# Another written-out order for a one-core attention and expert kernel

## The chip, the cores and the metric

The kernel runs on one core of a Trainium2 chip. A core has a matrix engine (TensorE, PE in the profile; its weight loads are PEld), VectorE (DVE), ScalarE (ACT), GpSimd (POOL) and SyncE (SP). Each works through its own instructions in order; between engines, instructions wait for semaphores. Transfers between the off-chip memory and the on-chip memory (SBUF) are started by instructions on SP, on POOL or on ScalarE, and run by themselves. TensorE writes its results to PSUM, which has eight banks here called P0 to P7. The metric is the device time of one execution in microseconds; lower is better.

## The reference

With 8 batches, 12 heads, 448 rows and a head width of 64:

```
scores = (q @ k^T) / sqrt(64)
attn   = max(scores, 0)**2 / 448
x      = (attn @ v), heads side by side        # 3584 x 768
h      = x @ w_in                              # 3584 x 2048
g      = h / (1 + exp(-1.702 h))
out    = g @ w_out                             # 3584 x 768, float32
```

All inputs are float32; the kernel computes its products in float16 with float32 sums.

## The kernel before, in words

The attention is cut into 24 units (a batch and four heads), numbered 0 to 23. The rest is cut into eight groups of tokens, g = 0 to 7, of 384 and 512 tokens in turn. A group can start when the units of its tokens are done. Most of the work of groups 1 to 7 uses a scheme with seven products in place of eight (Strassen's), which needs sums and differences of blocks: of w_in (`winS`), of w_out (`wT`), of x (`T`) and of g (`asum`).

The order of everything is written out by hand, as a list of 1950 words. The kernel reads the list from front to back and issues each word's instructions; each engine then runs its own in that order. A word has a name, numbers, after `:` the engine that does it (a ScalarE, d VectorE, p POOL), and after `@` the PSUM banks that it takes. Without a suffix `K`, `r`, `t` and `h` are on ScalarE, `Q` and `v` on POOL, and the others on VectorE (`home`). The words that matter here, with the lines of the code that they run:

- `Lk8`, `Lq8`: load k or q of unit 8 in float32 into `kst` / `qst` (one buffer each), on SP's queue (L99). `K8`, `Q8`: the cast to float16. `Rk8`, `Rq8`: a transposition by DMA on SP's queue into `kT` / `qT` (three tiles each, L119). `jk`, `jq`, `V`: a load that casts on the way, on POOL's queue (L104). In units 0 to 5, `tk`, `tq` transpose on TensorE instead (L131) and `ek`, `eq` copy the result.
- `s8.3`: the scores of block 3 of unit 8, four matmuls into two banks (L150). `r8.3.0`, `r8.3.1`: relu of the two banks into a float16 tile `at` (L161 on VectorE, L163 on ScalarE). `x8.3`: the square of that tile in place, 128 x 896 (L169 on ScalarE, L88 on VectorE or POOL). `a8`: attention times v for the whole unit, 28 matmuls, four for each of the seven blocks in order (L181). `e`: copies of its result into x.
- `jwa`, `jwb`, `jo`: loads of w_in and w_out, on POOL's queue. `S`, `W`, `T`, `A`: the sums of w_in, w_out, x and g, on VectorE (L88). All four read two tiles in SBUF.
- `f`: the plain first product of group 0 and part of group 1 (L228). `u`: one of the seven products for a block of w_in and a group, six matmuls into the banks `hx` (L203). `t`: a copy of such a bank into a float32 tile `gf` (five buffers, L79 or L83). `b`: bank plus `gf`. `g`: the activation into `gf` (ScalarE, L214). `v`: the step that scales `gf` and writes it as float16 into `ge` or `go` ("widen", L217).
- `p`: one of the seven products with w_out, eight matmuls into the banks `ox` (L203); `i`: a single of 16 matmuls for the odd tile of a group. `h`, `l`, `n`: copies and sums of their results into `osb`; `l` with last number 5 is a plain copy. `o`, `q`: stores.

A word that waits for its data holds up every later word on its engine, and on that engine alone. On POOL stand only words that read SBUF, and transfers.

## Time and profile before

| | |
|---|---|
| time, median of 3 runs | 368.98 us (368.62 to 369.25) |
| the profiled execution | span 372.2 us; the profile gives no other time for it |
| mean granted TensorE clock in it | 0.987 |
| busy time PE / DVE / ACT / POOL | 358.6 / 302.9 / 281.3 / 137.6 us |
| HBM read / written | 45.61 / 11.01 MB |
| last block of w_out landed | 66.2 us after the start |

The profile is one execution with every instruction's start and end on each engine. Besides a page with totals it answers questions: groups of instructions by line, engine and shapes (count, busy time, mean duration in ns, idle time before them and what ended it), who waited for whom, the chain of work that ended last, instructions in order of time, and the busy time of each engine in given stretches, followed there by the granted clock, the DMA share and GB/s. In the page's picture of 40 equal slices (9.3 us each) a digit is the busy share in tenths.

### The profile page before, as it was taken

To read this page: it belongs to the slowest core of one execution; us is meant where nothing else is said; L and a number is where in the kernel's file an instruction comes from. 1 tells how busy PE (TensorE), PEld (TensorE's weight loads), DVE (VectorE), ACT (ScalarE), POOL (GpSimd) and SP (SyncE) were. 2 spreads that over 40 slices of the span, in tenths; PEclk is the share of its full clock that TensorE was granted. 3 is DMA by queue.
4 is the path that set the end of the run, shared out by engine and by line. 5 is a ranking of instruction groups with operands and counts; after the bars stand their busy time and mean duration, and the time that the engine had idled before them with its cause. 6 is when DMAs were issued, how large, how long until landed. Compare 5 with 4: busy or idle time off the path is not lost.

```text
span 372.2 us, 9025 instructions
## 1 busy us (share of the span) xinstructions
PE 358.6 (96%) x3562; PEld 233.2 (63%) x3562; DVE 302.9 (81%) x556; ACT 281.3 (76%) x540; POOL 137.6 (37%) x202
## 2 busy tenths in 40 slices
PE   7699999799999999999999999999999999999994
PEld 4345554465559755786558755686559755688562
DVE  3988995899988989877998889898897899856552
ACT  3979985579989998798897898868887889346210
POOL 5859264714412732054411613344602421034300
PEclk9989999899999999999999999999999999999998
DMA  9999999918997791849965695784583242300334
GB/s 192 183 204 163 213 209 226 218 18 173 200 225 165 151 221 25 167 105 174 179 170 98 146 184 172 188 171 119 82 205 23 41 97 26 85 2 2 85 97 117
DMA packets 65226, 51.38 MB, mean 138 GB/s; under 512 B 35744, under 2 KB 61856, under 8 KB 65184
## 3 DMA queue, kind: packets, MB, share of 16 engines
q1 hardware_dynamic: 48176, 36.22, 43.2%
q0 software_dynamic: 16608, 14.09, 26.4%
q8 instruction: 28, 0.46, 0.5%
q10 hardware_dynamic: 400, 0.49, 0.4%
q14 instruction: 14, 0.11, 0.1%
HBM read 45.61 MB, written 11.01 MB: 152 GB/s over the span
## 4 chain that ended last, share of the span: by engine, by line
PE 84%; DMA 7%; DVE 3%; POOL 2%; ACT 1%; issue 1%; SPq 0%; DVEq 0%; ACTq 0%
PE ox L203 30%; PE hx L203 27%; PE sc L150 9%; PE av L181 8%; PE os L203 6%; DMA wout<-in_moe_w_out_dram 4%; PE ht L228 3%; DMA v<-in_v_dram 2%; DMA qst<-in_q_dram 1%; DVE wT L88 1%; PE tr L131 1%; POOL ge L217 1%; DVE at L88 1%; ACT gf L214 1%; POOL go L217 0%
## 5 line engine op out<-in xcount | busy, mean ns | idle before, releaser
L163 ACT ACTIVATE at<-sc 128x448 f16<-128x448 f32 x201 | 99.6, 559 | 13.0 <-PE sc L150 12.7
L161 DVE TENSOR_SCALAR at<-sc 128x448 f16<-128x448 f32 x135 | 79.8, 618 | 10.9 <-PE sc L150 10.6
L217 POOL TENSOR_SCALAR go<-gf 128x512 f16<-128x512 f32 x64 | 42.6, 665 | 79.1 <-ACT gf L214 75.7
L169 ACT ACTIVATE at<-at 128x896 f16<-128x896 f16 x72 | 68.2, 962 | 1.7 <-DVE at L161 1.2
L217 POOL TENSOR_SCALAR ge<-gf 128x384 f16<-128x384 f32 x64 | 35.4, 554 | 74.0 <-ACT gf L214 70.8
L203 PEld LDWEIGHTS <-win 128*128 128x128 f16 x624 | 56.7, 98 | 8.5 <-issue 2.4
L88 DVE TENSOR_TENSOR at<-at 128x896 f16<-128x896 f16 x92 | 55.9, 631 | 1.7 <-ACT at L163 0.6
L88 DVE TENSOR_TENSOR gf<-hx,gf 128x512 f32<-128x512 f32 (+1 forms) x78 | 47.7, 625 | 11.5 <-ACT gf L79 5.4
L150 PE MATMUL sc<-qT,kT 64*64 64x448 f16 x672 | 52.6, 363 | 1.3 <-DVE qT L83 0.6
L214 ACT ACTIVATE gf<-gf 128x512 f32<-128x512 f32 (+1 forms) x78 | 43.8, 585 | 11.7 <-DVE gf L88 11.6
L203 PEld LDWEIGHTS <-winS 128*128 128x128 f16 x468 | 43.4, 99 | 8.2 <-issue 3.9
L203 PE MATMUL ox<-wout,go 128*128 128x384 f16 x256 | 46.4, 326 | 0.0
L203 PEld LDWEIGHTS <-go 128*128 128x128 f16 x320 | 29.9, 98 | 23.2 <-issue 5.8
L203 PE MATMUL hx<-T,winS 128*128 128x256 f16 (+1 forms) x312 | 38.2, 268 | 2.7 <-DVE gf L83 2.7
L181 PE MATMUL av<-at,v 64*64 64x448 f16 x672 | 37.5, 357 | 1.0 <-DMA v<-in_v_dram 1.0
L203 PEld LDWEIGHTS <-ge 128*128 128x128 f16 x256 | 24.0, 98 | 18.4 <-issue 4.1
L150 PEld LDWEIGHTS <-kT 64*64 64x64 f16 x672 | 18.7, 106 | 26.3 <-issue 22.1
L79 ACT ACTIVATE gf<-hx 128x384 f32<-128x384 f32 (+1 forms) x44 | 23.3, 537 | 15.4 <-PE hx L203 12.0
L203 PE MATMUL ox<-wT,asum 128*128 128x384 f16 x192 | 34.9, 327 | 0.0
L203 PE MATMUL hx<-xo,win 128*128 128x256 f16 x252 | 31.4, 273 | 0.4 <-ACT gf L79 0.4
L203 PEld LDWEIGHTS <-asum 128*128 128x128 f16 x224 | 21.1, 98 | 16.3 <-issue 3.3
L81 ACT ACTIVATE osb<-ox 128x384 f32<-128x384 f32 x32 | 15.4, 496 | 19.2 <-PE ox L203 19.1
(75 smaller groups left out, 475.9 us busy)
## 6 DMA issues: line engine op xcount, KB each, us to landing
out_dram<-osb SPq DMA_DIRECT2D x52, 192.0 KB, 3.2
kst<-in_k_dram SPq DMA_DIRECT2D x19, 448.0 KB, 4.7
qst<-in_q_dram SPq DMA_DIRECT2D x19, 448.0 KB, 4.9
v<-in_v_dram POOLq DMA_DIRECT2D x24, 224.0 KB, 5.6
win<-in_moe_w_in_dram POOLq DMA_DIRECT2D x8, 384.0 KB, 9.7
wout<-in_moe_w_out_dram POOLq DMA_DIRECT2D x4, 768.0 KB, 11.5
...
```

Source lines behind the costliest of these rows:

```text
L79: nc.scalar.activation(out=o, in_=i, func=AF.Copy)
L81: nc.scalar.activation(out=o, in_=i, func=AF.Copy, scale=scale)
L88: eng[e].tensor_tensor(out=o, in0=x, in1=y, op=op)
L150: nc.tensor.matmul(out=sc[a][c, 0:S], lhsT=st["kT"][r, j, c], rhs=st["qT"][r, :, c], start=True, stop=True)
L161: nc.vector.tensor_scalar(out=o, in0=i, scalar1=0.0, scalar2=None, op0=ALU.max)
L163: nc.scalar.activation(out=o, in_=i, func=AF.Relu)
L169: nc.scalar.activation(out=at, in_=at, func=AF.Square)
L181: nc.tensor.matmul(out=av[s][64 * a:64 * a + 64, 0:S], lhsT=v16[r, a, 64 * j:64 * j + 64], rhs=at[r, a, :], start=(j == 0), stop=(j == J - 1))
L203: nc.tensor.matmul(out=o, lhsT=lhs(i), rhs=rhs(i), start=start and i == 0, stop=i == n - 1, skip_group_check=True)
L214: nc.scalar.activation(out=o, in_=i, func=AF.Gelu_apprx_sigmoid, scale=1.0 / SC)
L217: eng[e].tensor_scalar(out=o, in0=i, scalar1=SC, scalar2=1.0, op0=ALU.mult, op1=ALU.mult)
L228: nc.tensor.matmul(out=hp[g, f][:, 0:n], lhsT=w[:, i, fo:fo + 128], rhs=xts[g][:, i, 0:n], start=i == 0, stop=i == NK - 1)
```

## The change

The list of words is replaced by another list of the same 1950 words. Each name with its numbers is there exactly once in both. What differs is the order, the engine suffixes and the bank numbers. No operation is added or taken out, and no tile changes its size or its number of buffers.

By engine suffix, the words that change most are these:

| word | before | after |
|---|---|---|
| `x` square (168) | 92 VectorE, 72 ScalarE, 4 POOL | 58 VectorE, 42 ScalarE, 68 POOL |
| `r` relu (336) | 201 ScalarE, 135 VectorE | 212 ScalarE, 124 VectorE |
| `v` widen (128) | 128 POOL | 92 POOL, 36 VectorE (19 of 384 columns, 17 of 512) |
| `K` cast (19) | 7 ScalarE, 3 VectorE, 9 POOL | 4 ScalarE, 3 VectorE, 12 POOL |
| `Q` cast (19) | 9 POOL, 9 ScalarE, 1 VectorE | 4 POOL, 9 ScalarE, 6 VectorE |
| `l` 5 copy (12) | 8 ScalarE, 4 VectorE | 1 ScalarE, 11 VectorE |
| `e` copy of attention (72) | 40 ScalarE, 32 VectorE | 38 ScalarE, 34 VectorE |

Of the four loads of w_out, `jo0.0`, `jo0.1`, `jo1.1`, `jo1.0` is the order before; after, it is `jo1.0`, `jo0.0`, `jo1.1`, `jo0.1`, and the last two stand later in the list. Of the first loads, `V0` and `V1` stand ahead of `jwb2`.

The diff, cut to the stretches that are spoken of (lines of the list between them left out):

```diff
@@ -465,182 +465,180 @@
         two["z"] = zeros
         words = (
-            "jq1 z13@0 Lk0 I K0:d tk0@1 ek0 z1 Lq0 Q0:a tq0@2 tq1@3 jk1 eq0 s0.1@4.5 jwb2 jk2 "
-            "s0.6@6.7 s0.4@0.1 r0.4.0:d r0.6.0 tk1@2 ek1 jq2 jq3 eq1 s0.3@6.0 r0.1.1 r0.4.1 "
-            "r0.1.0 x0.1 s0.0@5.2 r0.0.0 s0.2@1.4 r0.2.0:d r0.3.1:d r0.3.0 s0.5@3.5 r0.6.1 "
-            "s1.1@6.1 r0.2.1 r0.0.1:d s1.2@7.0 s1.5@4.2 x0.0 r0.5.0 r1.1.1 r1.2.1 jk3 x0.4 "
-            "r0.5.1:d tq2@3 r1.2.0 x0.2 x0.6:a x0.5 x0.3 V0 r1.5.1 s1.0@1.0 x1.2 tk2@7 r1.5.0:d "
-            "r1.0.0 ek2 tk3@5 r1.0.1 jwa0 s1.3@2.1 eq2 r1.1.0 x1.1:a V2 a0@0.6 V1 x1.5:a r1.3.1 "
-            "s1.4@4.7 ek3 r1.3.0 jq4 jwb0 s2.1@3.5 r1.4.1 e0.0.1 s2.2@1.2 r1.4.0:d jk4 e0.0.0 "
...
-            "r3.3.0 r3.2.0 f0.3.1 V3 ek4 f0.2.1 f0.0.0@6 s3.0@5.3 a2@2.7 e2.0.0 r3.0.0 S2.1 "
-            "r3.0.1 x3.0:a e2.0.1:a s3.1@4.5 r3.1.0 f0.1.0@3 f0.0.1 f0.1.1 f0.1.2 e2.1.0:a g0.1 "
...
-            "s4.6@4.6 s4.4@7.5 jo0.0 eq5 f0.10.0@0 r4.4.0:d f0.10.1 f0.10.2 x4.0 v0.8 e3.0.0:a "
-            "r4.6.1:d r4.4.1 f0.7.0@2 s5.4@1.7 e3.0.1:a s4.5@5.3 r4.6.0 g0.10 s5.1@4.6 v0.10 "
...
-            "a4@0.1 r5.0.0:d r5.0.1:d g0.7 g0.11 jo0.1 v0.11 s5.6@2.5 r5.2.1 r5.2.0 s5.5@4.6 "
...
-            "f0.15.0@2 f0.15.1 r5.5.0 f0.14.0@3 x5.6 f1.1.0@7 jo1.1 f0.14.1 x5.5 v0.4 x5.1:a "
-            "f0.9.1 v0.2 S3.1 jo1.0 f0.9.2 g0.9 v0.9 f0.13.0@4 f0.13.1 f0.12.0@6 f0.12.1 f1.3.0@5 "
-            "e4.0.0:a S2.2 x5.4 Lq6 f0.15.2 Lk6 x5.0:a x5.3:a S2.3 S1.1 x5.2 f1.7.0@1 f0.14.2 "
-            "g0.14 f0.12.2 g0.15 g0.12 S3.2 f1.7.1 f0.13.2 f1.5.0@0 Q6:d f1.0.0@3 f1.1.1 S2.4 "
-            "g0.13 v0.13 a5@2.6 v0.15 e5.0.0 K6 e5.0.1:a Lk7 v0.14 S1.2 f1.0.1 f1.5.1 T1.1 "
-            "f1.4.0@4 T1.2 v0.12 f1.7.2 S3.3 T1.4 W2.1 W0.1 f1.5.2 g1.7 v1.7 f1.6.0@2 A0.0.1@0 "
-            "Lq8 g1.5 W3.1 f1.4.1 f1.4.2 g1.4 W2.2 f1.0.2 g1.0 Rk6 Rq6 v1.5 v1.0 f1.6.1 f1.3.1 "
-            "u1.2.0@6 f1.2.0@1 t1.2.0 f1.1.2 W1.1 f1.3.2 K7 Rk7 u1.3.0@0 u1.2.1@4 g1.3 g1.1 v1.1 "
-            "v1.3 Q8:a v1.4 f1.6.2 f1.2.1 f1.2.2 g1.2 v1.2 p0.0.0@3 h0.0.0 V8 b1.2.1 t1.3.0:d "
-            "u1.3.2 u1.2.2 u1.2.3 Lk8 V6 W2.4 W0.2 T1.3 W2.3 g1.2.1 g1.6 t1.2.2 K8:p s6.0@5.7 "
-            "s6.2@1.2 v1.2.1 r6.0.0 W1.2 u1.2.4 W3.2 r6.2.1:d r6.0.1 r6.2.0 t1.2.4 x6.0:a W3.3 "
-            "u1.3.1@5 p0.0.1@2 W3.4 b1.3.1 A0.0.2@1 Lq7 s6.1@7.1 u1.2.5 b1.2.3 r6.1.1 r6.1.0:d "
-            "l0.0.1 u1.3.3 u1.2.6 s6.3@1.7 W0.4 x6.1:a p0.0.2 W1.3 b1.2.6 Rq8 g1.2.3 r6.3.0:d "
...
-            "i0.2.0@2 K11:p r8.1.1 r7.6.0 x7.2 Lq10 x7.5:a x7.6 S1.3 r8.0.1 S0.3 s8.2@6.7 "
-            "r8.2.0:d r8.1.0 a7@5.1 s8.3@4.0 o0.1 e7.0.1 Rk9 Rq9 x8.1 r8.3.0:d x8.0 n0.2.0:a "
-            "Q10:a r8.2.1 e7.1.1 A1.0.1@0 s8.6@2.6 x8.2:a r8.3.1 i0.2.1@7 r8.6.0 r8.6.1 x8.3:a "
-            "h1.0.0 V11 s8.5@0.4 e7.0.0 r8.5.0 x8.6 s8.4@2.1 r8.4.0 r8.4.1 A1.0.2@1 r8.5.1:d "
-            "p1.0.1@6 n0.2.1:a x8.4 p1.0.2 e7.1.0:a Lk10 s9.0@0.2 s9.1@1.4 r9.0.0:d r9.1.1:d "
-            "l1.0.1 x8.5:a r9.0.1 r9.1.0 a8@7.5 s9.3@2.0 S1.4 x9.0 r9.3.0:d e8.0.0:a K10:p "
...
-            "s12.0@7.3 r12.0.0 l2.0.1 r12.0.1 r12.2.1:d a11@5.6 e11.0.1:a r12.2.0:d e11.0.0:a "
-            "x12.0 s12.1@1.7 s12.4@0.3 T3.1 T3.2 r12.1.0:d r12.4.1 p2.0.3 r12.1.1 A2.0.3 u3.0.0@6 "
...
-            "s13.1@2.1 a12@5.0 r13.1.0:d g3.3.3 r13.3.1:d r13.3.0 r13.1.1 g3.3.1 v3.3.1 b3.3.6 "
...
-            "s16.6@4.2 b4.3.6 h3.2.2 l3.2.1 s17.0@7.0 r16.6.1:d x16.0:a r16.5.0 r16.6.0 r16.5.1 "
-            "r17.0.0:d x16.4:a A3.2.4 g4.3.3 x16.6 x16.5 o3.1 p3.2.4 r17.0.1 p3.2.3 Lq20 o3.0 "
-            "s17.3@3.2 g4.3.6 r17.3.1 x17.0 Lk19 v4.3.6 v4.2.5 s18.1@4.7 K19:p Rk19 h3.2.4:d "
-            "l3.2.3 r18.1.0 r17.3.0 a16@5.0 e16.0.0 s17.1@2.4 r17.1.0 e16.0.1 p3.2.6 r17.1.1 "
...
-            "A7.2.1@1 A7.0.4 A7.2.2@0 A7.2.3 p7.2.2 h7.2.2 l7.2.1 p7.2.3 A7.2.4 p7.2.4 o7.1 "
-            "q7.2.0.0 p7.0.6 h7.2.4 l7.2.3 q7.3.1.0:a q7.2.0.1:a l7.0.6 o7.0 p7.2.5 l7.2.5:d "
-            "q7.3.0.0:a q7.3.0.1 q7.3.1.1:a p7.2.6 l7.2.6 q7.2.1.0:a q7.2.1.1"
...
+            "jq1 I z13@0 z1 Lk0 K0 tk0@1 ek0 jk1 tq1@2 eq1:a V0 jk2 Lq0 Q0:d tq0@3 eq0 tk1@4 ek1 "
+            "s0.4@5.6 r0.4.1:d r0.4.0 s0.2@7.0 V1 s0.1@1.2 r0.2.1:d jwb2 s0.6@3.4 r0.2.0 r0.6.1 "
+            "s1.5@5.6 r0.1.0 r1.5.1 r0.6.0:d s0.5@7.0 r0.5.0:d jq2 tk2@4 s0.3@3.1 r1.5.0 r0.5.1 ek2 "
+            "s1.3@6.7 x0.4 r0.3.1 s0.0@5.4 r0.0.1 jq3 jk3 jwb0 jwa0 r0.3.0 r0.0.0:d s1.2@0.1 r1.2.0 "
+            "r1.2.1 x0.2 r0.1.1:d s1.0@5.4 r1.0.1:d r1.3.0 V2 r1.3.1 jk4 x0.0 x0.5:p r1.0.0 "
+            "s1.1@3.0 tq2@2 x0.3:p x0.1 x1.5:a x0.6 s1.6@1.4 a0@6.7 jq4 x1.2 r1.1.0 eq2 s2.1@5.3 "
+            "r1.6.1 x1.3 r1.6.0 r1.1.1:d tk3@2 ek3 x1.1 e0.0.0:a tq3@4 eq3 jwa1 r2.1.0 s1.4@1.0 "
...
+            "x2.4 x2.1 x2.5:a tq4@2 x2.3 eq4 r3.3.1 a2@1.6 e2.1.0:a e2.0.1:a x3.3:p s3.1@2.5 r3.1.1 "
+            "ek4 e2.0.0 V5 f0.1.0@7 f0.1.1 e2.1.1 f0.3.2 g0.3 Lk6 f0.2.2 r3.1.0 f0.1.2 g0.2 jo1.0 "
...
+            "jo0.0 a3@1.4 r4.0.1:d r4.6.0 s4.5@6.5 s5.4@0.7 r4.0.0 x4.0 f0.5.0@3 r4.6.1 x4.1 f0.5.1 "
+            "f0.10.0@2 x4.6 r5.4.1 x4.2:p r5.4.0 r4.5.1 f0.9.0@7 f0.5.2 g0.5 f0.9.1 f0.9.2 x5.4:p "
...
+            "x5.3:a x5.2:p f1.2.0@3 v0.3:d x5.6:a v0.6 jo1.1 S2.2 Rq6 f1.7.0@1 g0.13 S3.2 v0.13 "
+            "f1.7.1 x5.5 a5@5.0 e5.0.1 e5.0.0:a f1.5.1 f1.2.1 f1.3.2 g1.3 f1.2.2 g1.2 jo0.1 "
+            "f0.7.0@6 f0.7.1 v0.12 v1.3 T1.1 T1.2 f1.7.2 f1.5.2 v1.2 S2.3 f0.7.2 g1.7 Lq8 g1.5 v1.5 "
+            "Lk7 s6.0@2.5 r6.0.0:d r6.0.1 g0.7 s6.5@0.4 r6.5.0 s6.6@3.1 r6.6.0 r6.6.1:d f0.15.0@7 "
+            "f0.15.1 f0.15.2 v0.7:d u1.2.0@5 r6.5.1:d g0.15 s6.3@2.6 v0.15 r6.3.0 S0.2 v0.10:d "
+            "s6.2@1.0 s6.4@3.7 r6.2.0 r6.4.0:d u1.3.1@4 W0.1 u1.3.0@2 t1.2.0 u1.2.2 r6.3.1 f1.4.0@1 "
+            "f1.6.0@3 S3.3 t1.3.0:d u1.3.2 b1.3.1 f1.0.0@6 f1.0.1 T1.4 f1.0.2 t1.2.2 f1.6.1 f1.6.2 "
+            "r6.4.1 g1.0 v1.7 A0.0.1@0 v1.0 Q8 t1.3.2:d g1.3.1 x6.6:a A0.0.3 A0.0.2@1 Lq7 r6.2.1:d "
+            "x6.2:a f1.1.0@7 f1.1.1 f1.4.1 u1.2.1@6 g1.6 v1.3.1 W1.1 K7 T1.3 f1.4.2 W0.2 v1.6 W1.2 "
+            "W3.1 u1.2.4 Lk8 g1.4 Rk7 b1.2.1 x6.0:a W3.2 t1.2.4:d g1.2.1 u1.3.3 p0.0.0@0 h0.0.0 "
+            "u1.2.3 v1.4 Q7:a W0.3 W2.1 W2.2 x6.4:p u1.3.4 v1.2.1 f1.1.2 g1.1 v1.1 S3.4 t1.3.4 "
+            "x6.3:a x6.5 p0.0.1@3 p0.0.2 S2.4 b1.3.3 g1.3.3 b1.2.3 g1.2.3 V10 W2.3 v1.2.3 Rq7 "
+            "v1.3.3 u1.3.6 V6 h0.0.2 u1.2.6 u1.2.5 g1.2.5 W1.3 W3.3 Lq9 s7.4@1.7 r7.4.1 p0.0.4 "
...
+            "s8.6@7.6 r7.2.1:d x6.1 x7.2:p x7.0:a a6@4.5 v1.2.6:d l0.0.5:a v1.2.5 r8.6.1 r7.1.0 "
+            "r7.1.1 p1.0.0@0 l0.0.6 o0.0 V12 x7.5 e6.1.1:a e6.1.0:a e6.0.0:a A0.2.5@0 s8.1@3.6 K9:p "
+            "x7.1:p o0.1 s7.6@2.1 r8.6.0 r7.6.1:d Rk9 r7.6.0:d e6.0.1:a x7.6:p r8.1.1 S1.2 s7.3@4.7 "
+            "r7.3.1 r7.3.0:d x7.3 h1.0.0:d i0.2.0@5 S1.4 r8.1.0 x8.1:a s8.3@6.1 r8.3.1:d n0.2.0 "
+            "g1.3.6 s8.0@7.2 r8.3.0 a7@3.4 r8.0.0 e7.1.0 r8.0.1 Lk11 e7.0.0 v1.3.5:d s8.4@6.7 "
+            "r8.4.0 r8.4.1 x8.4:a s8.2@1.2 r8.2.0 e7.1.1 x8.6:p r8.2.1:d V11 e7.0.1:a i0.2.1@5 "
+            "A1.0.1@1 A1.0.3 s8.5@3.6 r8.5.1 Q10:a A1.0.2@0 Rq9 s9.0@7.2 K11:d Rk11 p1.0.1@1 "
+            "n0.2.1:a p1.0.2 r8.5.0 x8.5:a Lq11 s9.3@4.6 h1.0.2 r9.0.0:d r9.0.1:d s9.1@7.5 r9.3.1 "
+            "r9.1.1 T2.1 r9.3.0:d r9.1.0:d x8.3:p x8.2:p x8.0:p a8@2.3 e8.1.0:a v1.3.6 S1.3 e8.0.1 "
...
+            "s9.5@5.0 r9.5.1 s9.6@4.2 v2.1.3 r9.6.0 A1.2.3 u2.2.5 A1.2.2@1 u2.3.1@3 r9.6.1 Rq10 "
+            "u2.3.4 b2.3.1 g2.3.1 p1.0.6 g2.2.5 u2.3.3 x9.6:p r9.5.0 Rk10 s10.3@0.4 x9.2 v2.3.1:d "
+            "l1.0.6 s10.0@2.6 t2.3.4 b2.3.3 r10.3.0 g2.3.3 v2.3.3 Rq11 s10.1@5.1 r10.1.0:d "
...
+            "p1.2.6 x11.3:p K13:d v2.2.5 x11.5 s12.4@0.7 r12.4.1 r12.3.0:d s12.2@5.6 r12.4.0 "
+            "x11.1:p a11@1.2 Rk14 e11.0.1:a Q14:a x12.4:p Lk16 K16:p l1.2.6 o1.2 s12.1@3.7 "
+            "r12.2.0:d r12.2.1:d e11.0.0 s12.5@5.0 r12.5.1 u3.1.0@6 Lq15 r12.5.0 r12.1.0:d u3.0.1@2 "
...
+            "s13.1@3.6 x12.3:p r13.1.1:d r13.1.0:d K15:p g3.3.3 Rk15 x12.6:p a12@2.1 v3.3.5 "
...
+            "e13.1.1 x14.3:p s14.5@0.1 r14.5.0:d r14.5.1 s14.6@4.7 p3.0.0@3 V19 Rq15 e13.0.0 "
+            "p3.0.1@2 e13.0.1:a r14.6.0 r14.6.1 x14.6:p s14.4@1.5 Q16:d Rq16 x14.5:a s15.3@0.4 Lq18 "
+            "o2.1 r14.4.1 e13.1.0 h3.0.0:d r15.3.0 l3.0.1 r14.4.0 s15.0@7.6 r15.0.1:d x14.4:a "
+            "r15.3.1:d r15.0.0:d K18:p p3.0.2 x15.3:p s15.2@5.0 r15.2.0 r15.2.1:d a14@6.1 g3.3.6 "
...
+            "e15.0.0:a V16 x16.4:a r16.5.0 r16.5.1:d l3.2.1 s17.1@3.6 s17.0@7.0 x16.1:p r17.0.0 "
+            "x16.5:a x16.2 p3.2.4 r17.1.1:d h3.2.4 r17.1.0:d p3.2.3 Rq18 K19:p r17.0.1 x17.0:a "
+            "s17.3@4.5 r17.3.0 r17.3.1:d s17.2@7.6 x16.0:p r17.2.0:d l3.2.3 a16@0.3 r17.2.1 "
...
+            "p7.0.4 g7.2.6 v7.2.6:d p7.2.1@7 A7.2.1@1 A7.2.2@0 h7.0.4 l7.0.3 A7.2.3 h7.2.0:d l7.2.1 "
+            "p7.0.5 l7.0.5 o7.1 q7.2.0.0 p7.2.2 h7.2.2 p7.0.6 p7.2.4 A7.2.4 p7.2.3 q7.2.0.1:a "
+            "h7.2.4 p7.2.5 l7.0.6 o7.0 l7.2.3 q7.3.1.0:a q7.3.1.1:a l7.2.5:d p7.2.6 q7.3.0.0:a "
+            "q7.3.0.1 l7.2.6 q7.2.1.0:a q7.2.1.1"
...
         ).split()
         for w in words:
             do(w)
```

## The prediction

> **What bounds the kernel now.** I read the page's busy times first, then its slices, then the stretches around the places where TensorE is not full.
>
> ```profile
> PE 358.6 (96%) x3562; PEld 233.2 (63%) x3562; DVE 302.9 (81%) x556; ACT 281.3 (76%) x540; POOL 137.6 (37%) x202
> ...
> PE   7699999799999999999999999999999999999994
> ...
> POOL 5859264714412732054411613344602421034300
> PEclk9989999899999999999999999999999999999998
> ```
>
> PE is the bound, full from slice 3 on, with one dip in slice 7. POOL is the idle engine. The stretches put numbers on it:
>
> ```profile
> 1.00:30.00 29.00, 24.40 (x316) 12.90 (x316) 21.48 (x41) 21.47 (x44) 20.25 (x24) 0.94 1.17 201
> 30.00:68.00 38.00, 37.92 (x369) 21.07 (x369) 30.13 (x55) 31.30 (x62) 20.47 (x32) 1.00 1.19 201
> 68.00:76.00 8.00, 5.29 (x32) 3.25 (x33) 8.00 (x12) 2.80 (x5) 6.04 (x7) 0.79 0.98 208
> 76.00:170.00 94.00, 94.00 (x949) 63.05 (x948) 83.22 (x155) 85.07 (x161) 32.30 (x48) 1.00 0.74 145
> ```
>
> From 76 us PE is never short: no order can win anything there, it can only lose. What can be won lies before 30 us and at 68 to 76 us, where PE stands 2.71 us and then runs at a reduced clock. The waits and the timeline say why:
>
> ```profile
> DVE wT L88 <- DMA wout<-in_moe_w_out_dram: 3.9, 1, 3.9
> PE hx L203 <- DVE gf L83: 2.7, 1, 2.7
> ```
>
> ```profile
> 72.12 1.34 POOL L83 CAST k<-kst 128x896 f16<-128x896 f32 x1
> 72.13 1.74 DVE L88 TENSOR_TENSOR wT<-wout,wT 128x768 f16<-128x768 f16 x2
> 72.26 2.89 PE L203 MATMUL hx<-T,winS 128*128 128x256 f16 x14 [2.71 <-DVE gf L83]
> ```
>
> VectorE stood on `W2.1` until the last block of w_out had landed (66.2 us); the snap that PE needed was queued behind it. The same lines show a second thing: a VectorE operation with two SBUF inputs takes 1.28 us (the longest of the eight wT operations; the shortest is 0.54) beside a POOL cast. A cast of kst took 0.91 instead of 0.62 us on VectorE beside a POOL widen. The two engines hold each other up. Last, the prices, and how long a DMA transposition (of q) takes:
>
> ```profile
> L163 ACT ACTIVATE at<-sc 128x448 f16<-128x448 f32 x201 | 99.6, 559 | 13.0 <-PE sc L150 12.7
> L169 ACT ACTIVATE at<-at 128x896 f16<-128x896 f16 x72 | 68.2, 962 | 1.7 <-DVE at L161 1.2
> L88 DVE TENSOR_TENSOR at<-at 128x896 f16<-128x896 f16 x92 | 55.9, 631 | 1.7 <-ACT at L163 0.6
> L217 POOL TENSOR_SCALAR ge<-gf 128x384 f16<-128x384 f32 x64 | 35.4, 554 | 74.0 <-ACT gf L214 70.8
> L88 POOL TENSOR_TENSOR at<-at 128x896 f16<-128x896 f16 x4 | 7.1, 1800 | 3.4 <-ACT at L163 3.4
> ```
>
> ```profile
> DMA to landing us min/median/max: 2.9/5.6/7.6
> ```
>
> **The change, part by part.** Durations are from this execution (span 372.2 us; the three unprofiled runs have a median of 368.98, 0.9% less). I work in differences against the span and add their sum to the median.
>
> *Who does what.* Counted over both lists: squares go from 92 VectorE / 72 ScalarE / 4 POOL to 58 / 42 / 68; widens from 128 POOL to 92 POOL and 36 VectorE; relus on VectorE from 135 to 124; POOL's casts from 18 to 16; the last copies (`l` 5) move 7 from ScalarE to VectorE. ScalarE loses 30 x 0.947 + 7 x 0.48 + 3 K casts x 0.96 and gains 11 relus x 0.496 (busy time by count): about -29 us. POOL gains 64 x 1.80 = 115, loses 36 x 0.61 = 22: 137.6 to 229 us. A widen on VectorE is in no row. It is bounded by the copy gf<-hx of its size (0.56 and 0.69 us) and by the line through two f16 outputs of VectorE, 64 elements 0.219 and 896 elements (cast of kst) 0.62, which gives 0.35 and 0.42. I take the latter, the same kind of source: 19 x 0.35 + 17 x 0.42 = 14 us (22 at the other end), and 7 `l` 5 (3.9) and 5 Q casts (3.1), against 34 squares (21) and 11 relus (6.5) saved: 302.9 to about 298.
>
> PE's instructions are the same. The chain shows their pieces (8 ox matmuls in 1.30 us, 28 av in 1.32), so a pair product is 1.30, a single 2.60, attn-v 1.32, scores 0.19, a unit product 0.50 or 0.655, a first-matmul part 0.34 or 0.45: 336 us. "PE sum" below is this sum up to a word.
>
> *The w_out wait goes: -4.4 us (bounds 0 and -4.4).* The gap is 2.71 us, and the 3.4 us after it run at half clock (1.7 us). In the new list the first `W` stands at PE sum 49.7 instead of 46.8. PE runs 13.6 us behind its sum here (attn-v of unit 5: sum 43.7, start 57.3), so it falls due at 63.3 us and needs jo1.0 and jo0.0. POOL has 37.7 us of work up to the second of these, and stood still for 9.2 us before the matching issue of before (POOL sum 27.2, issue 36.4). So it issues at 39 to 47 and lands, at 9.4 to 14.7 us, by 48 to 62. jo1.1 (POOL sum 49.1) lands by 60 to 70 and is due at 70.8; jo0.1 (50.5) by 61 to 74, due at 75.2. All in time, the last ones narrowly. I take -4.4.
>
> *The start: +1 us (bounds -1.7 and +5.6).* Up to unit 5's attn-v VectorE and ScalarE lose 8.8 us of work together, PE 2.5 us: (8.8 / 2 - 2.5) x 0.92 = 1.7 us to win at most. But POOL's sum there goes from 35.5 to 49.6 us, with 13 squares among the DMA issues; it begins at 1.25 us, and a5 would be due at 57.3 - 2.5 = 54.8. If POOL waits only for tile slots as before (about 4.5 us in the first 14), its last square ends at 55.4; if all its 9.2 us recur, at 60. The nearest is the slot waits: about 1 us late. V0's DMA moves ahead of jwb2; that takes away the 1.0 us that PE waited for v at 17.70, inside the same sum.
>
> *Squares that come late: +6.4 us (bounds 0 and 15).* From unit 6 on, 55 squares are on POOL. Take a8. Counting from a7's first matmul, PE has a7 1.32, six scores 1.14, one single 2.60, two pair products 2.60: a8 starts at 7.66. POOL has x8.6, V11 (0.74), x8.3, x8.2, x8.0: 4 x 1.80 + 0.74 = 7.94 after x7.6, which ends at -0.2 if POOL is free for it and at +2.1 behind K9 and x7.1. So x8.0, the first that a8 reads, is 0.1 to 2.4 us late. The same sum, POOL's queue in its order against PE's sum, gives for the later units: a7 1.0, a8 2.4, a11 0.3, a12 0.6, a14 0.5, a16 1.3, a19 0.1, a20 0.2 late, the others 0.3 us or more early: 6.4 us. With the 1.67 us of the shortest POOL square it is 4 us. Before, such a square took 0.63 us on VectorE and PE waited for none. Behind each late a-word stand the evacuations (`e`) and then x, so PE stands; nothing else can move up on it.
>
> *VectorE waiting for POOL: inside the same 6.4 (0 to 15).* 215 VectorE operations of the new list read two SBUF inputs, or a float32 one, that is 0.64 per us of PE. If they fall as they come, a POOL square of 1.8 us holds one up for 0.63 us on average. Before, VectorE lost by rows (mean less minimum) 5.9 us, of 10.6 that the same formula gives for 128 widens and 18 casts; scaled so, 0.35 us a square. Its words summed by row x 0.93 (the rows of all words make 325, the page says 302.9, as instructions overlap) plus this, between attn-v words: a5 to a8 46.3 us where PE has 46.0, a8 to a11 38.1 and 37.7, a11 to a14 (13 squares) 45.4 and 43.0, a14 to a17 39.6 and 39.0, then less than PE: 3.7 us over. Unscaled it is 15 us. These are the stretches in which the squares are late too, so I do not add them; 15 is the upper end.
>
> *Transpositions that come late: +3.0 us (bounds 0 and 9).* SP's 94 DMAs stand in another order too. kT has three tiles; Rk10 takes the one that unit 9's scores read to the end, and from s9.6 to the first scores of unit 10 PE has four unit products, a pair product and s9.6 itself, 3.5 us. kT's median is 5.2 us: 1.9 late with the issue (0 at 3.0, 5.1 at 8.6). Q16, a VectorE cast, stands 5.1 us ahead of unit 16's first scores: 0.61 + 5.6 is 1.1 late (0 to 4). Rq9, queued on SP behind Rk9 and so behind POOL's K9, comes 1 to 2 us late, inside a8's 2.4. Before, the tightest place had 7.7 us for the tile (unit 21) and 6.2 for the cast, and PE did not wait. The v loads and the other casts stand as far ahead as before, or POOL's sum has room.
>
> After unit 23 there is no square on POOL, and the last words are the same pair products, copies and stores but for their order: 0.
>
> Sum: -4.4 + 1 + 6.4 + 3.0 = +6.0 us, 375.0.
>
> *Two rules of the Trainium skill.* POOL's square has 4 rows at 1.80 us against 0.61 on VectorE, 3 to 1. "GPSIMD Engine Reference", section "Engine selection", puts two-input elementwise work there at about 2 to 1; by an estimate from it a square would take 1.2 us, no a-word would be late, and the sum would be 368.6. I keep the row. The clock fell to 0.79 in the stretch with a 2.71 us gap and stayed 1.00 around one of 0.39. "TensorE: Matmul & The Clock Gate", part 1, names an idle window of about 3.4 us; by it no stall here would cost clock, by the row one of 2.4 us might, at 1.7 us.
>
> **The rivals.** *The stalls are absorbed.* For it: before, VectorE was held up by up to 0.7 us at a time and PE lost 0.4 us in all after 76 us; POOL may run ahead of its place in the list; a-words read their squares one by one. Against: the a8 sum and the tile of Rk10. Only the wait at 68 to 76 us then counts. It decides where PE's new waits after 76 us come to less than 4.4 - 0.7 (0.2%) = 3.7 us, 0.2 us a unit, with the start unchanged. Time 363 to 368.2, about 366.
>
> *VectorE becomes the bound.* For it: a11 to a14 is over PE's time even at the small price. Against: before, it held 98% of PE's time from a5 to a8. At the 15 us price: 368.98 - 4.4 + 1 + 15 = 380.6, with the transpositions 383.6.
>
> *w_out is late again*, behind POOL's squares: the 4.4 us stay, 379.4; the upper part of the forecast's band.
>
> **How the numbers follow.** A measurement tells about 0.2% from no change. Forecast (369.8 to 379.5): 0.51. Absorbed: 0.24. VectorE bound (above): 0.18. Within 0.2%: 0.07. So faster 0.24, same 0.07, slower 0.69. The range runs from -4.4 - 1.7 + 0 + 0 (362.9) to -4.4 + 5.6 + 15 + 3 (388.2), that is 363 to 388; the forecast's own is 369.8 to 379.5.
>
> **What would show it.** No wait of PE for a gf tile near 70 us, clock 1.00 there. POOL's `at<-at` row x68 near 1.8 us. New waits of av matmuls for POOL's at, most at a8 and a16, and of sc matmuls for a transposition at units 10 and 16. VectorE's at<-at row with a maximum near 2 us. ScalarE near 252, POOL near 229 us busy. I am wrong if PE's av words never wait, if POOL's squares take under 1.5 us, or if VectorE's widens take 0.6 us.

## The result and the profile after

The changed kernel takes 422.39 us (419.66 to 424.55, 6 runs), the kernel before 369.12 us beside it: a ratio of 1.143, 95% interval 1.138 to 1.147. The change makes it 53 us slower. The forecast was 375.0 us, with a range that ended at 388.

The page of the changed kernel: busy times, and three of its slices.

```profile
PE 377.4 (90%) x3562; PEld 240.2 (57%) x3562; DVE 365.3 (87%) x561; ACT 258.9 (62%) x509; POOL 229.9 (55%) x228
...
PE   7799788987977898999889899899998997999995
...
DVE  3998987998899999999999989979999888796472
...
PEclk9799969997888999999998999999999998999998
```

ScalarE (252 forecast) and POOL (229 forecast) are where they were expected. VectorE is not: 365.3 us in place of the forecast 298. TensorE has dips over the whole length, where it had one. The stretches that were shown of before, now of after (length; busy time and instructions of PE, PEld, DVE, ACT, POOL; granted clock; DMA share; GB/s):

```profile
1.00:30.00 29.00, 24.43 (x285) 13.42 (x286) 22.55 (x36) 19.53 (x41) 24.53 (x30) 0.88 1.13 196
30.00:68.00 38.00, 31.86 (x331) 16.09 (x329) 33.86 (x46) 22.97 (x48) 25.11 (x24) 0.91 0.79 136
68.00:76.00 8.00, 8.00 (x68) 4.33 (x65) 6.01 (x12) 6.22 (x14) 4.78 (x7) 1.00 1.21 245
76.00:170.00 94.00, 80.20 (x718) 48.84 (x716) 89.13 (x127) 57.66 (x116) 55.86 (x52) 0.93 0.64 133
```

At 68 to 76 us TensorE is full at clock 1.00, and neither it nor VectorE waits for w_out: that wait is gone, as forecast. (By the prediction's sum TensorE is about 12 us further behind here than in the profile of before, so these lines alone don't show that the new order of the loads did it.) But from 76 to 170 us it works 80.2 of 94 us where it was never short, and VectorE is busy for 89.1 us of them. The groups of instructions name the cause (count, busy us, mean ns, then idle time):

```profile
L88 POOL TENSOR_TENSOR at<-at 128x896 f16<-128x896 f16 x68 | 119.1, 1762 | 50.4 <-DVE at L161 23.5 <-ACT at L163 18.5 <-DVE xo L83 3.9
L88 DVE TENSOR_TENSOR at<-at 128x896 f16<-128x896 f16 x58 | 61.9, 1082 | 1.0 <-ACT at L163 0.3
L217 DVE TENSOR_SCALAR go<-gf 128x512 f16<-128x512 f32 x17 | 15.0, 899 | 1.3 <-ACT gf L214 1.3
```

POOL's squares take about what they took before (1.76 us, 1.80 before). It is VectorE's squares that went from 631 to 1082 ns, the longest to 4.46 us. I add up, over VectorE's instructions, the time above the shortest of the same group (less 20 ns for each): 75.9 us after, 5.9 before. I call this VectorE's hold-up below. Relus from PSUM (612 ns, 618 before) and sums of a PSUM bank with a float32 tile (622, 625 before) have no part in it.

How a hold-up becomes a loss of TensorE's time, in the timeline of the changed kernel (start, length, engine, operation; in brackets the idle time ahead and what ended it):

```profile
111.60 4.95 POOL L88 TENSOR_TENSOR at<-at 128x896 f16<-128x896 f16 x3
...
112.60 4.37 DVE L88 TENSOR_TENSOR winS<-winS,win 128x768 f16<-128x768 f16 x1
...
116.89 0.61 DVE L161 TENSOR_SCALAR at<-sc 128x448 f16<-128x448 f32 x1
117.56 2.58 PE L181 MATMUL av<-at,v 64*64 64x448 f16 x26 [2.50 <-DVE at L161]
```

Three squares run on POOL. A sum of w_in on VectorE, 0.55 us when nothing is in its way, lasts until 0.4 us after the third is over. The relu behind it, which POOL itself doesn't lengthen (0.61 us), comes 3.8 us late, and TensorE stands for 2.50 us. So it is with most of TensorE's waits: of the 36.9 us in waits of over 0.15 us the trace puts 33.5 down to VectorE, 2.7 to a load of q, 0.7 to ScalarE and none to POOL. The three longest sums, with the count and the longest wait:

```profile
PE sc L150 <- DVE at L161: 7.9, 9, 3.2
PE ox L203 <- DVE asum L88: 4.2, 2, 3.0
PE av L181 <- DVE at L88: 3.0, 3, 1.6
```

In all TensorE stands 38.5 us up to its last matmul (8.8 before), and its instructions, the same 3562, take 377.4 us in place of 358.6.

### The profile page after: what moved, and what is told of

The parts are those of the page before. It is cut to its first block, busy times and chain, and to the rows that moved or that the text cites. A ratio compares the mean times of both kernels' runs of the same rounds, so it can differ in the third digit from the quotient of the medians.

```text
span 420.5 us, 9074 instructions
## 1 busy us (share of the span) xinstructions
PE 377.4 (90%) x3562; PEld 240.2 (57%) x3562; DVE 365.3 (87%) x561; ACT 258.9 (62%) x509; POOL 229.9 (55%) x228
## 3 DMA queue, kind: packets, MB, share of 16 engines
q0 software_dynamic: 16608, 14.09, 22.5%
## 4 chain that ended last, share of the span: by engine, by line
PE 45%; DVE 39%; issue 7%; ACT 5%; DMA 3%; POOL 1%; DVEq 0%; SPq 0%; ACTq 0%; POOLq 0%
PE hx L203 16%; PE ox L203 15%; DVE at L161 8%; DVE at L88 8%; PE av L181 5%; PE sc L150 4%; DVE gf L88 3%; DVE wT L88 2%; DVE asum L88 2%; DVE winS L88 2%; DMA q<-in_q_dram 2%; PE os L203 2%; ACT at L163 2%; PE ht L228 2%; DVE osb L85 2%
## 5 line engine op out<-in xcount | busy, mean ns | idle before, releaser
L88 POOL TENSOR_TENSOR at<-at 128x896 f16<-128x896 f16 x68 | 119.1, 1762 | 50.4 <-DVE at L161 23.5
L161 DVE TENSOR_SCALAR at<-sc 128x448 f16<-128x448 f32 x124 | 72.5, 612 | 11.1 <-PE sc L150 11.0
L150 PE MATMUL sc<-qT,kT 64*64 64x448 f16 x672 | 58.3, 373 | 12.3 <-DVE at L161 7.9
L217 POOL TENSOR_SCALAR go<-gf 128x512 f16<-128x512 f32 x47 | 33.4, 711 | 63.6 <-ACT gf L214 45.7
L88 DVE TENSOR_TENSOR at<-at 128x896 f16<-128x896 f16 x58 | 61.9, 1082 | 1.0 <-ACT at L163 0.3
L181 PE MATMUL av<-at,v 64*64 64x448 f16 x672 | 42.8, 379 | 7.2 <-DVE at L88 3.0
L217 POOL TENSOR_SCALAR ge<-gf 128x384 f16<-128x384 f32 x45 | 26.2, 583 | 38.0 <-ACT gf L214 33.9
L169 ACT ACTIVATE at<-at 128x896 f16<-128x896 f16 x42 | 39.5, 953 | 5.5 <-DVE at L161 5.1
L79 ACT ACTIVATE gf<-hx 128x512 f32<-128x512 f32 (+1 forms) x45 | 24.2, 543 | 20.4 <-PE hx L203 14.3
L181 PEld LDWEIGHTS <-v 64*64 64x64 f16 x672 | 22.9, 112 | 20.8 <-issue 12.4
## 6 DMA issues: line engine op xcount, KB each, us to landing
win<-in_moe_w_in_dram POOLq DMA_DIRECT2D x8, 384.0 KB, 10.6
```

The source lines that it names most:

```text
L79: nc.scalar.activation(out=o, in_=i, func=AF.Copy)
L88: eng[e].tensor_tensor(out=o, in0=x, in1=y, op=op)
L150: nc.tensor.matmul(out=sc[a][c, 0:S], lhsT=st["kT"][r, j, c], rhs=st["qT"][r, :, c], start=True, stop=True)
L161: nc.vector.tensor_scalar(out=o, in0=i, scalar1=0.0, scalar2=None, op0=ALU.max)
L169: nc.scalar.activation(out=at, in_=at, func=AF.Square)
L181: nc.tensor.matmul(out=av[s][64 * a:64 * a + 64, 0:S], lhsT=v16[r, a, 64 * j:64 * j + 64], rhs=at[r, a, :], start=(j == 0), stop=(j == J - 1))
```

## The experiments

The theory (T1): a square on POOL keeps VectorE out of operations with two SBUF inputs, and that costs the time. The rivals: the order and the banks cost it, whoever does the squares (R1); or the squares are merely late, since POOL is slow (R2).

**Squares back on their old engines, in the new order.** Every `x` word of the new list gets its old suffix:

```diff
-  x0.5:p  x0.3:p  ...  x6.4:p
+  x0.5    x0.3    ...  x6.4
```

> The changed kernel's order and banks, with every square back on the engine it had before (92 VectorE, 72 ScalarE, 4 POOL). T1 (POOL's squares keep VectorE from its operations with two SBUF inputs): VectorE's time over the shortest of each group falls from 75.9 us to under 15 us and the time to 365 to 378 us. R1 (the order and the banks cost the time, whoever does the squares): over 400 us. R2 (the squares are merely late, as POOL is slow): also 365 to 378 us, so this run parts R1 from the other two only.

Measured: 413.0 us, ratio 1.114 (1.106 to 1.122); hold-up 13.8 us. The hold-up is nearly gone and the time hardly moved. On its face that is R1, and T1's number fails. But the run does two things: 34 squares come back to VectorE and 30 to ScalarE, at places of a list that left no room for them there. The waits of TensorE in this run say so:

```profile
PE av L181 <- ACT at L169: 5.9, 6, 2.1
PE sc L150 <- DVE at L161: 3.8, 6, 1.7
PE av L181 <- DVE at L88: 2.6, 2, 1.7
```

**Squares moved, in the old order.** The opposite: the old list with the new suffixes of `x`.

```diff
-  x1.1:a  x0.3    ...
+  x1.1    x0.3:p  ...
```

> The order of before, with every square on the engine that the changed kernel gives it (68 on POOL). T1: the hold-up of VectorE rises from 5.9 us to 50 us or more, and the time to 395 to 425 us. R1: within 6 us of before, 363 to 375. R2: over 380 us, with PE's waits mostly for POOL's squares and VectorE's hold-up under 20 us.

Measured: 426.9 us, ratio 1.152 (1.145 to 1.158); hold-up 39.5 us. TensorE also waits 14.0 us for POOL's squares and 7.4 for v, whose loads queue on POOL. Neither T1's 50 us nor R2's picture comes out clean.

**Extra work for POOL that nobody needs.** In the old list, behind 65 squares:

```diff
+        scratch = const("scratch", [128, 352])
+        def spare(e, p, u, j):
+            for a in range(2):
+                tt(scratch, slots[u, j][:, a, 0:352], slots[u, j][:, a, 0:352], ALU.mult, "p")
+        two["y"] = spare
```

> The kernel before, and 65 extra words on POOL, each right behind one of the squares that the change moves: two multiplications of 128 x 352 of the finished square into a tile that nobody reads. No engine but POOL waits for them, apart from the square's tile, which comes free a little later. T1: VectorE is held up by 40 us or more in place of 5.9, and the kernel is 20 to 50 us slower though nothing needs the results. R2 (late results): within 4 us of before, 365 to 373.

Measured: 428.7 us, ratio 1.157 (1.150 to 1.165); hold-up 30.1 us, under T1's 40, and 59 us slower, over its 50. It looked like support for T1 until its twin:

**The same without reading SBUF.** Each extra word reads 8 columns, to wait as before, and then fills the spare tile.

```diff
-            for a in range(2):
-                tt(scratch, slots[u, j][:, a, 0:352], slots[u, j][:, a, 0:352], ALU.mult, "p")
+            x = slots[u, j][:, 0, 0:8]
+            tt(scratch[:, 0:8], x, x, ALU.mult, "p")
+            for _ in range(4):
+                nc.gpsimd.memset(scratch, 1.0)
```

> The kernel before, with the 65 extra words on POOL again (428.7 us with multiplications that nobody needs), but each now reads 8 columns of the square, so that it waits for it as before, and then fills the spare tile four times, about 1.7 us, reading nothing. T1: 370 to 385 us, VectorE's hold-up under 15 us. If the 59 us came from POOL's own queue (widens, casts and loads behind the extra words): over 410 us.

Measured: 434.6 us, ratio 1.172 (1.163 to 1.181); hold-up 7.0 us. T1's number fails here. With hardly any hold-up the old order loses as much. Its loads of v stand behind the extra words on POOL's queue, and the longest sum of TensorE's waits in this run is for v:

```profile
PE av L181 <- DMA v<-in_v_dram: 19.7, 4, 8.7
```

So these two runs say nothing about the new list, only that the old one has no room on POOL.

**Order alone, engines alone.** The new list with all old suffixes, and the old list with all new ones.

> The changed kernel's order and banks, with every operation on the engine it had before. T1: the order by itself costs little; 362 to 376 us, VectorE's hold-up under 15 us, no wait of PE near 70 us. R1: over 400 us.

> The order of before with every operation on the engine that the change gives it. The squares alone gave 426.9 us, the new order with the old engines 457.2, both together (the change) 422.4. If order and engines only add up, this run is near 334 us, which the 358.6 us of TensorE's work rules out. If each order suits only its own engines, it is over 410 us; if the moves other than the squares' relieve VectorE, 385 to 410.

Measured: 457.2 us, ratio 1.233 (1.226 to 1.241), and 468.3 us, ratio 1.264 (1.255 to 1.272); hold-ups 14.2 and 58.4 us. T1's 362 to 376 us for the first fails too. Each half of the change by itself costs more (87 and 97 us) than both together (53). Order and engines can't be priced apart: each list holds only for the engines it was written for. To find the cause, the new list has to keep its engines, and only what the squares do may change. That is the next pair.

**POOL's squares cut to almost nothing.**

```diff
+        elif e == "p":
+            tt(at[:, :, 0:16], at[:, :, 0:16], at[:, :, 0:16], ALU.mult, e)
```

> The changed kernel with its 68 squares on POOL cut to 2 x 16 of 2 x 448 columns; the other columns are left unsquared. Nothing else changes. It takes away both what POOL's squares do to VectorE and what they delay. If POOL's squares are the whole cause (T1 or R2), the time falls to 360 to 378 us and VectorE's hold-up to under 15 us. If the order and the rest of the engines cost the time (R1), it stays over 400 us; between, the part that is gone is the squares' part.

Measured: 376.9 us, ratio 1.015 (1.008 to 1.023); hold-up 9.4 us. R1 falls: with the squares' work gone, the new order and all its other engines cost 1.5%, not 14%.

**POOL as busy as before, but reading nothing.**

```diff
+        elif e == "p":
+            for _ in range(2):
+                nc.gpsimd.memset(at, 1.0)
```

> The changed kernel with each square on POOL replaced by two fills of the same tile with ones, which write and read nothing; the squares of these tiles are left out. By the one fill in the profile (128 x 128 in 0.22 us, against 0.11 for one column) two should take about 1.8 us, like the square. So POOL is as busy and the tiles are as late, but no SBUF is read. T1 (VectorE is kept out): VectorE's hold-up falls from 75.9 to under 15 us and the time comes close to that of the kernel with the squares cut, 362 to 385 us. R2 (late squares): within 10 us of the changed kernel, 412 to 432.

Measured: 375.9 us, ratio 1.015 (1.008 to 1.021). The page and the groups of this run:

```profile
PE 358.5 (96%) x3562; PEld 233.8 (63%) x3562; DVE 311.0 (83%) x561; ACT 258.4 (69%) x509; POOL 223.4 (60%) x296
```

```profile
L172 POOL MEMSET at<- 128x896 f16 x136 | 116.7, 865 | 27.7 <-ACT at L163 10.8 <-DVE at L161 9.0 <-ACT xo L79 1.5
L88 DVE TENSOR_TENSOR at<-at 128x896 f16<-128x896 f16 x58 | 35.7, 631 | 1.4 <-ACT at L163 0.6
L220 DVE TENSOR_SCALAR go<-gf 128x512 f16<-128x512 f32 x17 | 10.8, 643 | 1.4 <-ACT gf L217 1.3
```

The fills take 116.7 us where the squares took 119.1, so a tile is finished as late as in the changed kernel. VectorE's squares are back at 631 ns, its busy time fell by 54 us, the hold-up from 75.9 to 19.9 us, and the time by 46.5 us. Late tiles cost nothing that shows against the run with the squares cut. R2 falls and T1 holds for the changed kernel: 46.5 of the 53 us are VectorE being kept out.

**Half of the squares filled.** Every second square on POOL becomes two fills.

```diff
+    turn = iter(range(68))
...
+        elif e == "p" and next(turn) % 2:
+            for _ in range(2):
+                nc.gpsimd.memset(at, 1.0)
```

> The changed kernel with every second of its 68 squares on POOL replaced by two fills (as in the run with all of them filled, 375.9 us); those 34 tiles are left unsquared. If each square's hold-up of VectorE goes into the time at about the same rate, 34 squares cost half of 46.5 us: 395 to 403 us, VectorE's hold-up 42 to 54 us. If VectorE has slack that has to be used up first (the prediction's reckoning, stretch by stretch), the first half costs less: under 392 us.

Measured: 390.4 us, ratio 1.054 (1.046 to 1.061); hold-up 42.4 us. From none to 34 squares the time rises by 14.5 us (0.43 each), from 34 to 68 by 32.0 (0.94 each). The first half costs less, as in the second case of the expectation. In part that is because it holds VectorE up for less: 22.5 us more than with all of them filled, and the second half 33.5 us on top (in this run a fill stands between any two squares on POOL). But a microsecond of hold-up also costs less time, 0.64 us in the first half and 0.95 in the second, which fits slack that is used up first. The three runs share one list, so they can be laid side by side. From unit 2's attention on, by stretch between attention words (POOL's squares in the list there; then the length of the stretch with all squares filled, with half of them filled, and in the changed kernel, in us, and in brackets VectorE's hold-up; "end" is TensorE's last matmul):

```
stretch     squares   filled         half           changed
a2 to a5       8      25.0  (1.6)    26.5  (4.4)    33.6 (10.1)
a5 to a8       9      52.4  (8.0)    60.2 (11.5)    66.5 (17.9)
a8 to a11      9      41.0  (3.0)    41.6  (4.6)    44.8  (9.0)
a11 to a14    13      45.2  (4.2)    46.5  (5.7)    52.2 (12.3)
a14 to a17     9      41.3  (2.0)    42.8  (5.4)    45.3  (8.2)
a17 to a20     9      43.9  (0.3)    44.1  (2.7)    46.8  (8.7)
a20 to a23     6      38.9  (0.5)    41.1  (2.7)    44.2  (4.4)
a23 to end     0      50.8  (0.3)    50.8  (0.3)    50.8  (0.4)
```

Ahead of a2, with five squares, it is 30.7, 31.8 and 31.8 us. In the changed kernel every stretch with squares loses, the one without loses nothing.

**Squares in four pieces.** If the way were merely held for one instruction, shorter ones should help.

```diff
+        elif e == "p":
+            for a in range(2):
+                for c in range(0, S, 224):
+                    o = at[:, a, c:c + 224]
+                    tt(o, o, o, ALU.mult, e)
```

> The changed kernel with each of the 68 squares on POOL made in four instructions of 128 x 224 in place of one of 128 x 896; the work is the same and nothing is left out. If a POOL instruction keeps VectorE out only until it ends, a VectorE operation now waits 0.5 us at most: hold-up under 35 us in place of 75.9, the time 380 to 400 us, longest square on VectorE under 1.8 us. If VectorE stays out while POOL's instructions follow each other, nothing gets better: hold-up over 60 us, time 415 to 440.

Measured: 418.3 us, ratio 1.132 (1.127 to 1.137); hold-up 55.9 us: between the two expectations, with the time on the side of "nothing gets better". Its groups:

```profile
L88 POOL TENSOR_TENSOR at<-at 128x224 f16<-128x224 f16 x272 | 167.9, 649 | 13.4 <-ACT at L163 9.6 <-DVE xo L83 1.4 <-POOL k L83 0.5
L88 DVE TENSOR_TENSOR at<-at 128x896 f16<-128x896 f16 x58 | 52.8, 926 | 1.8 <-ACT at L163 1.1
```

VectorE gains a little, but now POOL waits for VectorE after each piece: 167.9 us for the same squares, and TensorE waits 6.4 us for them. A few VectorE operations were passed over by up to 11 pieces in a row (6.48 us for the sum of w_in shown above).

**The two engines by themselves.** Twelve blocks of plain operations, nothing of the kernel:

```diff
+        BLOCKS = [(d_square, 12, None, 0), (d_square, 12, p_square, 6), (d_square, 12, p_split, 6),
+                  (d_square, 12, p_spaced, 6), (d_square, 12, p_fill, 12), (d_square, 12, p_widen, 16),
+                  (d_relu, 12, p_square, 6), (d_add, 12, None, 0), (d_add, 12, p_square, 6),
+                  (d_widen, 16, None, 0), (d_widen, 16, p_square, 6), (d_widen, 16, p_fill, 12)]
```

> No part of the computation; twelve blocks in which VectorE and POOL each work through a row of operations on tiles of their own, ScalarE starting both together. VectorE has 12 squares of 128 x 896 alone; then beside POOL's 6 squares, 6 squares in four pieces, 6 squares with a fill behind each, 12 fills, 16 widens; 12 relus from PSUM beside 6 squares; 12 sums of a PSUM and a float32 SBUF tile of 512 columns alone and beside 6 squares; 16 widens of 512 columns alone, beside 6 squares, beside 12 fills. If an instruction of POOL gives the way free at its end, VectorE gets an operation in after each POOL square, and 12 squares beside 6 take about 12 x 0.61 + 6 x 1.68 us, alternating from the start. If VectorE stays out while POOL's follow each other, its first square behind the start waits for all six, about 10 us, and the others then take 0.61. Fills, and relus from PSUM, should not hurt.

VectorE was not held back at the start of each block, so some rows met another row of POOL than meant; the groups are therefore taken over stretches of time in which one pair ran. First squares alone, then beside POOL's squares, then beside fills:

```profile
L41 DVE TENSOR_TENSOR vy<-vx 128x896 f16<-128x896 f16 x12 | 7.5, 625 | 0.6 <-ACT vx L81 0.3
...
L41 DVE TENSOR_TENSOR vy<-vx 128x896 f16<-128x896 f16 x7 | 12.5, 1789 | 0.5 <-ACT vx L81 0.3
L54 POOL TENSOR_TENSOR py<-px 128x896 f16<-128x896 f16 x6 | 11.7, 1954 | 13.9 <-ACT vf L81 13.5
...
L41 DVE TENSOR_TENSOR vy<-vx 128x896 f16<-128x896 f16 x12 | 7.5, 626 | 0.7 <-ACT vx L81 0.3
```

Relus from PSUM and sums of PSUM and a float32 tile, both beside POOL's squares, and then VectorE's widens beside squares and beside fills:

```profile
L44 DVE TENSOR_SCALAR vy<-acc 128x448 f16<-128x448 f32 x12 | 7.5, 624 | 14.9 <-ACT acc L81 14.6
...
L50 DVE TENSOR_TENSOR vy<-acc,vf 128x512 f16<-128x512 f32 x12 | 8.3, 691 | 3.2 <-ACT acc L81 2.9
...
L47 DVE TENSOR_SCALAR vy<-vf 128x512 f16<-128x512 f32 x7 | 11.1, 1590 | 0.2
...
L47 DVE TENSOR_SCALAR vy<-vf 128x512 f16<-128x512 f32 x13 | 13.8, 1062 | 0.7 <-ACT vf L81 0.3
```

With squares on both sides the engines take turns, one operation each, and a VectorE square beside a POOL square lasts 1.98 us (the one in seven that fell outside is 0.62): 1.36 us lost for every square of POOL. Fills, PSUM relus and PSUM sums cost nothing. A widen on VectorE, 0.43 us alone, lasts 1.78 us beside a square and 1.03 us beside a fill (the means above mix in rows at the edges of their stretch). In the run with fills the widens are 8 of the 19.9 us that stay: 36 of them, each about 0.23 us above the shortest on average. Squares beside POOL's widens were not caught here. Beside squares in four pieces the engines take turns as well, 0.86 us a VectorE square and 0.94 us a piece: four pieces cost VectorE 0.96 us in place of 1.36, and POOL 3.7 us in place of 1.95.

**Coming late to the row.** VectorE first does one to five relus and then four squares, beside a row of POOL's that has begun:

```diff
+            for _ in range(relus):
+                relu()
+            for t in vx:
+                square(nc.vector, t)
```

> No part of the computation; eight blocks. POOL starts a row of 6 squares in place on tiles of its own (in the last three blocks 6 widens of 512 columns); VectorE does 1 to 5 relus from PSUM first (0.62 us each, which POOL does not disturb) and then 4 squares of its own, so that it comes to POOL's row at different points. If it is always let in at the next end of a POOL instruction, its first square takes 0.6 to 2.3 us wherever it comes, and the engines then take turns. If it may be passed over, first squares of 3 us and more show up, as the 3.3 to 4.5 us of the changed kernel.

The first squares took 1.06, 2.13, 1.47, 0.82 and 1.80 us, all let in at the end of the POOL square they met, then turns of 2.10 us. Beside POOL's widens, 1.02 us a square (0.62 alone). No square was passed over. What makes VectorE miss its turn in the kernel was not found and stays open. Of 9 of its operations that began beside a square of POOL with another right behind it, 3 were passed over. Two more, the longest of all among them (4.46 us, from 48.09 us on), began while POOL issued a load and lasted until after two squares; no run here parts the issue from the squares.

**The loads of w_out in the new order, in the old list.**

```diff
-  ... jo0.0 ... jo0.1 ... jo1.1 ... jo1.0 ...
+  ... jo1.0 ... jo0.0 ... jo1.1 ... jo0.1 ...
```

> The kernel before with the four loads of w_out in the changed kernel's order (jo1.0, jo0.0, jo1.1, jo0.1) at the old places, nothing else. If the wait at 68 to 76 us is for the block that comes last, as read, it goes: 3 to 4.4 us faster than before. If the wait moves to the next sum of w_out, within 1 us of before.

Measured: 369.68 us, ratio 1.0005 (0.9984 to 1.0026). The 2.71 us gap is gone from the profile, VectorE no longer waits for w_out (3.85 us at once in the first profile of before), and the median has not moved. With V0 first as well:

```diff
-  ... jwb2 jk2 ... V0 ...
+  ... V0 jwb2 jk2 ...
```

> As the run before, and the first load of v ahead of the second half of w_in, as in the changed kernel. TensorE waited 1.0 us for this v at 17.7 us: another 0 to 1.0 us faster; if the halves of w_in then come late for the first products, slower by up to 2 us.

Measured: 371.0 us, ratio 1.0025 (0.9999 to 1.0052). Nothing is won; no version here beats the kernel before.

**The kernel before, profiled again.**

> The kernel before, unchanged, for another profile. The prediction took 4.4 us for the wait at 68 to 76 us, read from an execution of 374.1 us; the run with w_out in the other order lost that wait in its profile and no time in the median. If the wait is in some executions only, an execution of about 369 us shows no gap of over 1 us near 70 us. If it is always there, the gap of 2.7 us is there again, and the order of the loads merely moves the loss.

This execution took 368.5 us (span 366.8); the one that the prediction worked from had a span of 372.2, about 374 us with what lies around it. Its stretch at 68 to 76 us:

```profile
68.00:76.00 8.00, 7.50 (x69) 5.02 (x67) 8.00 (x14) 5.61 (x11) 3.60 (x5) 1.00 0.73 171
```

Gaps of 0.50 us, clock 1.00, and none of TensorE's waits goes back to w_out. VectorE still waits 1.85 us for its last block, but that wait ends at 62.34 us, and TensorE has work meanwhile. So the 4.4 us are not in this execution, which is near the median.

## Why the prediction was wrong

The sign was right, the size was not. The sign was in part luck: of the two terms that made it, squares that come late (+6.4 us) and transpositions that come late (+3.0), neither shows as a wait of TensorE in the changed kernel. Term by term:

*"VectorE waiting for POOL: inside the same 6.4 (0 to 15)"* is the step that failed. It priced a POOL square at 0.35 us of VectorE's time, scaled down from 0.63 because before showed only 5.9 of 10.6 us by rows. Measured, the 68 squares hold VectorE up by 56 us more than fills do (0.82 each), 70 us more than before in all (1.03 per square); two engines that always meet give 1.36. In the time it is 46.5 us. So the scaling was the error. The rows that it came from are of POOL's widens and casts, and a square is nearly three times as long as a widen; why widens and casts hold VectorE up for less than the formula says was not tested. How 0.63 was reached is not said either. At 0.64 operations per us that fall as they come, a square of 1.8 us holds up the first of them by 0.73 us on average, and by 1.04 us if every one that falls in it is counted; the measured 0.82 to 1.03 lies between the two.

The way from hold-up to time, stretch by stretch and only what exceeds TensorE's, did better than the price. With 0.82 to 1.03 us a square in place of 0.35 the prediction's four sums from a5 to a17 (3.7 us over, with 40 squares) give 22 to 31 us over; there the changed kernel is 28.9 us longer than the one with fills. That holds for the whole and not for each: a5 to a8 lost 14.1 us where the sum gives 4.5 to 6.4. And "then less than PE" failed: from a17 to a23, where the sum left room, the table shows a loss of 8.2 us, and up to a5, which this term left out, 9.7. An average over a stretch hides the single hold-up of 2 to 4 us that hits the relu behind it (112.60 us above), when TensorE has no other work ready.

*"Squares that come late: +6.4 us"*: wrong. The a8 sum took POOL's queue against TensorE's sum, and with fills of the same length the tiles are as late and cost nothing against cut squares (375.9 and 376.9 us). In the changed kernel no wait of TensorE for a POOL square shows; TensorE is itself late, and POOL catches up. Neither of the places named, a8 and a16, is among the attention words that wait.

*"The w_out wait goes: -4.4 us"*: the wait went, and in the old list the new order of loads takes it away too. The base was wrong. A wait of an execution of about 374 us was taken off the median of 369.0; in the second profile TensorE has none of it. The term is 0. The prediction's 0.9% sets a span against a time; in times it is 374 against 369, 1.4%, and of the 5.4 us between the two spans (372.2 and 366.8) 4.4 are that gap and the clock behind it.

Nor was the gap w_out's alone. Between the landing at 66.2 us and the copy that TensorE needed, four sums of VectorE ran beside POOL's widens. Two of them, in the first profile of before:

```profile
67.27 1.10 DVE L88 TENSOR_TENSOR asum<-ge 128x1024 f16<-128x1024 f16 x1
68.29 0.96 DVE L88 TENSOR_TENSOR wT<-wout,wout 128x768 f16<-128x768 f16 x1
```

The other two took 0.96 us as well. In the second profile the same four took 0.68 and three times 0.55 us. By these rows 1.65 of the 2.71 us are VectorE held up by POOL: what decided the change stood on TensorE's path in the profile of before already, and was read as a late load.

*"The start: +1 us (-1.7 to +5.6)"*: where TensorE reaches 47 us of its own work it is about 14 us further behind its sum than in the second profile of before, but about 3.5 with fills. So the start by itself lies inside its bounds, and VectorE's hold-up, which the term left out for these 13 squares, is the rest.

*"Transpositions that come late: +3.0 us"*: no wait of TensorE for a transposition shows in the changed kernel; the run with fills has 1.0 us. *Tail 0*: right, 50.8 us from a23 to the end in all three columns; before it is 49.9, with 0.7 us less work behind a23 by the prediction's sum.

With the measured terms: what the new order costs with fills, 1.5% or 5.4 us, and 46.5 us of hold-up make 52 of the 53 us. The 5.4 us were not taken apart further.

Of the rivals, "VectorE becomes the bound" was the one, with its mechanism and at a third of its price: it was given 15 us and 0.18. Its argument against was that VectorE held 98% of TensorE's time before from a5 to a8 (in the trace 43.2 of 47.5 us, 91%). So little room speaks for the rival: of the 56 us by which VectorE is held up more than with fills, 46.5 arrive in the time.

What the engines would show came out in part: clock 1.00 near 70 us, POOL's row x68 at 1.76 us. "VectorE's at<-at row with a maximum near 2 us" was where the error could be seen first: 4.46 us. One of the three signs of being wrong came: VectorE's widens took 0.67 and 0.90 us on average, where the shortest took 0.34 and 0.41.

The rule on engine selection would have made it worse still (368.6). The page that bore on the case was another: the Trainium skill, "SBUF — State Buffer", section "Who interferes with whom". It says that VectorE and GpSimd share a pair of ports that one instruction holds to its end, that a VectorE instruction with two SBUF inputs meets a GpSimd instruction that reads SBUF but not one that only writes, and that casts and tensor-scalar operations of VectorE can enter a two-port mode that meets either. The runs agree: 1.98 us beside a square, 626 ns beside fills, 1.03 us for a widen beside fills. The prediction had seen the same in before ("The two engines hold each other up") and priced it as a side effect.
